# One-row last piece of w4: sixteen loads of eight partitions in place of one load of 128

## The chip, the cores and the metric

The kernel runs on one core of a Trainium2 chip. The metric is the device time of one execution in microseconds; the runs of the kernel before took 406.42, 406.50 and 406.69 us (median 406.5).

## What is computed

One decode step of a block with two branches that share an input row x of 1024 values:

```python
x = A_x                                   # (1, 1, 1024)
xn = _layernorm(x)
return x + _A_ref(xn, ...) + _B_ref(xn, ...)
# A: q = xn @ wq, 32 query heads over 4 key/value heads, 65536 cached keys of width 128,
#    softmax(q k^T / sqrt(128)) v, then @ wo (4096 x 1024)
# B: h = gelu(layernorm(xn) @ w1), shifted by rows (with one row, zeros come in), @ w2, added to xn = x1;
#    x1 + gelu(layernorm(x1) @ w3) @ w4,   w3 1024 x 3584, w4 3584 x 1024
```

All tensors are bf16. The caches are 64 MB each, the weights the rest of 170 MB that are read once. With one row the shifted operand is all zeros, and the kernel takes the layer norm of x1 as that of xn; the w2 product is computed nonetheless.

## The kernel before

Everything that is read from memory comes through one list of `items` (lines 82 to 91), in the order of their use: two halves of wq, then for each of four key/value heads four tiles of 16384 keys (K) and values (V), with w3 and w1 put in between and a piece of wo behind each head, and at the end w2 and w4. w4 (28 rows of 1024 for each of 128 partitions) is cut by `W4_PIECES = (16, 8, 2, 1, 1)` into five pieces: 4 MB, 2 MB, 0.5 MB and twice 0.25 MB. The text calls them piece 0 to piece 4.

Each item is one load into one buffer ("slot") of a pool of five, issued on SP's queue by `issue` (line 98). Before item i is computed, `ensure(i + 4)` issues the loads up to four items ahead (lines 129 to 132, 441). A load into a slot waits for the reads of the item that had the slot five places before, and for that item's own load. So piece 4 is issued when the w2 matmuls are done, piece 3 when those of the last wo are.

A framework puts the waits in. It tells the completion of DMAs issued on SP and ACT by eight semaphores, lane 0 to lane 7, that are given out in turn: in the kernel before w2 has lane 3, pieces 0 to 4 have lanes 4, 5, 6, 7 and 0, and the two stores of the output lanes 1 and 2. A DMA that gets a lane again must wait on its queue until the lane's earlier DMA has landed, if nothing it has waited for before implies this.

`compute_w4` (line 326) adds the pieces' products to the two output rows in PSUM: for each row of a piece two matmuls by `row_acc` (line 160), 56 in all, which share the accumulator `psB` with the products of wo and w2. After piece 4, ACT casts one half of the result (line 336) and VectorE the other (line 337), and ACT and SP store them (lines 339, 340).

Of the kernel before, what the change touches and what calls it, by code (L numbers as in the profile page):

```python
# [18 lines left out]
W4_PIECES = (16, 8, 2, 1, 1)  # L19
# [3 lines left out]
def kernel(  # L23
# [14 lines left out]
    nc = tc.nc  # L38
    P = 128
# [10 lines left out]
    NOUT = A_wo.shape[1]  # L50
# [24 lines left out]
    w4_v = B_w4.rearrange("(m c) n -> m c n", c=FC)  # L75
# [4 lines left out]
    w4_start = [sum(W4_PIECES[:i]) for i in range(len(W4_PIECES))]  # L80
# [12 lines left out]
    st = {}  # L93

    def slot():
        return big.tile([P, KEYS], BF16, name="slot")

    def issue(item):
        kind = item[0]
        t = slot()  # L100
        if kind == "wq":
            src = wq_v[:, 4 * item[1]:4 * item[1] + 4, :].rearrange("p c n -> p (c n)")
        elif kind == "w3":
            src = w3_v[:, 4 * item[1]:4 * item[1] + 4, :].rearrange("p c n -> p (c n)")
        elif kind == "w4":
            c0 = w4_start[item[1]]
            src = w4_v[:, c0:c0 + W4_PIECES[item[1]], :].rearrange("p c n -> p (c n)")
        elif kind == "w1":
            src = w1_v
        elif kind == "w2":  # L110
            src = w2_v
        elif kind == "wo":
            src = wo_v[item[1]]
        else:
            cache = A_k_cache if kind == "K" else A_v_cache
            _, g, r = item
            src = cache[0, g, r * KEYS:(r + 1) * KEYS, :].rearrange("(p k) d -> p (k d)", p=P)
        nc.sync.dma_start(out=t[:, 0:src.shape[-1]], in_=src)
        st[item] = t
# [9 lines left out]
    def ensure(upto):  # L129
        while n_issued[0] <= min(upto, len(items) - 1):  # L130
            issue(items[n_issued[0]])
            n_issued[0] += 1
# [85 lines left out]
    for cg in range(4):  # L218
        nc.vector.tensor_copy(out=selbig[:, cg, :].rearrange("p (hl dd) -> p hl dd", dd=16),
                              in_=sel32[:, 8 * cg:8 * cg + 8].unsqueeze(2).to_broadcast([P, 8, 16]))  # L220
    sel8big = const.tile([P, P], F32, name="sel8big")
    nc.vector.tensor_copy(out=sel8big[:].rearrange("p (hl dd) -> p hl dd", dd=16),
                          in_=sel8[:].unsqueeze(2).to_broadcast([P, 8, 16]))
# [3 lines left out]
    for b in range(2):  # L227
        for par in range(2):
            nc.vector.tensor_copy(out=psel[:, 2 * b + par, :].rearrange("p (a i) -> p a i", a=4),  # L229
                                  in_=iv[:, b, par, :].unsqueeze(1).to_broadcast([P, 4, 32]))  # L230
# [242 lines left out]
```

## Time and profile before

| | before |
|---|---|
| runs (us) | 406.42, 406.50, 406.69 |
| profiled execution | 406.69 us, of which the span of its instructions is 404.8 |
| mean granted TensorE clock | 0.796 |
| PE busy | 245.7 us (61%), 1400 matmuls |
| VectorE busy | 215.7 us (53%) |
| ACT busy, POOL busy | 37.7 us, 11.2 us |
| moved by DMA | 170.11 MB, mean 420 GB/s over the span |
| first of the w4 matmuls, last of them, first cast of the output | 393.26, 400.76, 401.18 us |

Times in the views are microseconds from the start of the span. A line of the chain or the timeline has the start, the duration, the engine, the line of the kernel and the operation with its tiles (out<-in); "SPq" and "ACTq" are the queues that issue DMAs, and their durations are those of the issue, not of the transfer. "slot<-in_B_w_dram" are loads of w1 to w4. "DMA" in the page's rows is the mean busy share of sixteen DMA engines. A DMA of 128 partitions leaves sixteen semaphore updates in the trace, one for each engine that carried it; its landing is the last of them.

### The profile page before, as it was taken

What the parts mean: (1) busy time and instruction counts of PE and PEld (TensorE: products, weight loads), DVE (VectorE), ACT (ScalarE), POOL (GpSimd) and SP (SyncE); (2) the same over time, 40 slices, a digit from 0 to 9 for tenths busy, and PEclk for the clock granted to TensorE, in tenths of its full rate; (3) what the DMA queues carried; (4) which work ended last, traced back from release to release, by engine and by line L of the source; (5) the groups of instructions that cost most, each with busy time, mean ns of one, the idle gap of its engine ahead of it and who ended that gap; (6) DMA issues with size and microseconds to landing.
All of it is one profiled execution on the core that took longest, in us unless ns stands there. A gap on an engine that the chain in (4) does not pass through costs nothing.

```text
span 404.8 us, 3326 instructions
## 1 busy us (share of the span) xinstructions
PE 245.7 (61%) x1400; PEld 95.7 (24%) x1400; DVE 215.7 (53%) x235; ACT 37.7 (9%) x60; POOL 11.2 (3%) x30
## 2 busy tenths in 40 slices
PE   0385565328475847557657948384659474758456
PEld 0132222103132312112223313131233121213122
DVE  0419474017484848346665847475748383838500
ACT  0101101100201010120210010101010101010100
POOL 5001000000000000000010000000000000000000
PEclk9998878857795778768595868888958797679898
DMA  8999999999999999999999999999999999999993
GB/s 363 415 424 449 418 426 434 430 418 444 434 408 439 447 416 419 458 418 416 447 431 413 437 444 414 435 440 418 430 440 424 428 439 427 425 437 413 440 415 134
DMA packets 7065, 170.11 MB, mean 420 GB/s; under 512 B 1023, under 2 KB 1033, under 8 KB 1418
## 3 DMA queue, kind: packets, MB, share of 16 engines
q1 hardware_dynamic: 6772, 169.87, 98.0%
q8 instruction: 11, 0.18, 0.2%
q0 software_dynamic: 128, 0.02, 0.0%
q10 hardware_dynamic: 150, 0.01, 0.0%
q14 instruction: 4, 0.03, 0.0%
HBM read 169.88 MB, written 0.01 MB: 420 GB/s over the span
## 4 chain that ended last, share of the span: by engine, by line
DMA 54%; PE 23%; DVE 17%; ACT 2%; another core or an unknown queue 1%; issue 1%; DVEq 0%; ACTq 0%
DMA slot<-in_A_k_cache_dram 44%; DVE slot L353 11%; PE sc L357 10%; DMA slot<-in_B_w_dram 7%; PE psB L160 5%; PE oacc L389 4%; DMA x_bf<-in_A_x_dram 3%; DVE pT L377 2%; DVE mx L361 2%; ACT p_sb L374 2%; PE rows L244 1%; PE pm_e L417 1%; DVE m L365 0%; PE pm_mx L363 0%
## 5 line engine op out<-in xcount | busy, mean ns | idle before, releaser
L353 DVE STREAM_TRANSPOSE slot<-slot 128x2048 f32<-128x2048 f32 x64 | 142.3, 2281 | 61.1 <-DMA slot<-in_A_k_cache_dram 61.1
L357 PE MATMUL sc<-slot,qst 128*128 128x512 bf16 x512 | 131.6, 411 | 40.9 <-DVE slot L353 40.9
L389 PE MATMUL oacc<-slot,pT 128*32 128x512 bf16 x512 | 56.0, 616 | 48.0 <-DVE pT L377 48.0
L357 PEld LDWEIGHTS <-qst 128*128 128x128 bf16 x512 | 51.6, 103 | 125.1 <-issue 45.9
L361 DVE TENSOR_REDUCE mx<-sc 128x1 f32<-128x1024 f32 x16 | 19.6, 1225 | 34.7 <-PE sc L357 34.7
L374 ACT ACTIVATE p_sb<-sc,nball 128x1024 bf16<-128x1024 f32 x16 | 17.8, 1114 | 209.8 <-DVE nball L372 209.8
L389 PEld LDWEIGHTS <-pT 128*32 128x32 bf16 x512 | 17.5, 139 | 75.0 <-DVE pT L377 49.4
L377 DVE STREAM_TRANSPOSE pT<-p_sb 128x1024 bf16<-128x1024 bf16 x16 | 19.9, 1245 | 23.3 <-ACT p_sb L374 23.3
L244 PE MATMUL rows<-slot,xpad 128*32 128x512 bf16 (+1 forms) x144 | 13.6, 509 | 6.1 <-DMA slot<-in_B_w_dram 6.1
L363 PE MATMUL pm_mx<-ident_f,mx 128*1 128x128 f32 x16 | 4.3, 270 | 21.1 <-DVE mx L361 21.1
L160 PE MATMUL psB<-slot,oT 128*1 128x512 bf16 x64 | 12.6, 564 | 4.3 <-DVE oT L428 4.3
L394 ACT COPY ob<-oacc 128x512 f32<-128x512 f32 x12 | 7.0, 586 | 58.6 <-PE oacc L389 58.6
L160 PE MATMUL psB<-slot,dst_h 128*1 128x512 bf16 x56 | 7.9, 444 | 3.2 <-DMA slot<-in_B_w_dram 3.2
L370 PE MATMUL pm_mx<-ident_f,rep 1*128 1x1 f32 x16 | 3.5, 222 | 9.9 <-DVE rep L367 9.9
L417 PE MATMUL pm_e<-og,selbig 128*128 128x128 f32 x32 | 7.4, 403 | 3.4 <-DVE og L409 3.4
L244 PEld LDWEIGHTS <-xpad 128*32 128x32 bf16 x144 | 5.7, 127 | 15.0 <-issue 13.7
L172 PE MATMUL pm_ln<-ln_rowsum_a,ones_f 128*128 128x1 f32 x2 | 0.6, 348 | 13.6 <-DVE psel L229 13.6
L337 DVE CAST out<-psB 64x256 bf16<-64x256 f32 x1 | 0.4, 417 | 15.2 <-ACT out L336 15.2
L363 PEld LDWEIGHTS pm_mx<-ident_f,mx 128*1 128x1 f32 x16 | 1.3, 79 | 29.0 <-DVE mx L361 29.0
L417 PEld LDWEIGHTS pm_e<-og,selbig 128*128 128x128 f32 x32 | 6.3, 293 | 6.7 <-DVE og L409 6.7
L365 DVE TENSOR_REDUCE m<-pm_mx 1x8 f32<-1x128 f32 x16 | 4.4, 278 | 5.8 <-PE pm_mx L363 5.8
L374 ACT ACT_TABLE_LOAD x3 | 3.8, 1283 | 35.6 <-DVE nball L372 35.6
(97 smaller groups left out, 79.3 us busy)
## 6 DMA issues: line engine op xcount, KB each, us to landing
slot<-in_A_k_cache_dram SPq DMA_DIRECT2D x16, 4096.0 KB, 34.5
slot<-in_A_v_cache_dram SPq DMA_DIRECT2D x16, 4096.0 KB, 35.5
slot<-in_A_wq_dram SPq DMA_DIRECT2D x2, 4096.0 KB, 21.4
slot<-in_A_wo_dram SPq DMA_DIRECT2D x4, 2048.0 KB, 38.4
slot<-in_B_w_dram SPq DMA_DIRECT2D x2, 3584.0 KB, 42.6
slot<-in_B_w_dram SPq DMA_DIRECT2D x3, 2048.0 KB, 26.9
slot<-in_B_w_dram SPq DMA_DIRECT2D x1, 4096.0 KB, 27.8
slot<-in_B_w_dram SPq DMA_DIRECT2D x1, 512.0 KB, 16.1
```

The costliest lines, as they stand in the source:

```text
L160: nc.tensor.matmul(psB[32 * j:32 * j + 1, :], lhsT=lhsT, rhs=rhs, start=(not row_started[j]), stop=False, tile_position=(0, 32 * j), skip_ ...
L244: nc.tensor.matmul(acc[32 * j:32 * j + 32, bk, 0:width], lhsT=xp[:, c, :], rhs=wt[:, cl, ch * width:(ch + 1) * width], start=(c == 0), sto ...
L353: nc.vector.transpose(out=kf[:, cg, :], in_=kf[:, cg, :])
L357: nc.tensor.matmul(sc[:, hf, :], lhsT=qst[g % 2][:, o:o + 128], rhs=kr[:, cg, hf, :, bp // 2, :, bp % 2], start=(cg == 0 and bp == 0), sto ...
L361: nc.vector.reduce_max(out=mx[:], in_=sc[:].rearrange("p h n -> p (h n)"), axis=AX.X)
L363: nc.tensor.transpose(pm[0:1, 0:P], mx[:, 0:1], ident_f[:])
L365: nc.vector.reduce_max(out=m8[:], in_=pm[0:1, 0:P].rearrange("o (j h) -> o h j", h=8), axis=AX.X)
L374: nc.scalar.activation(out=p_sb[:], in_=sc[:], func=ACTF.Exp, bias=nball[:, r:r + 1], scale=SCALE, accum_out=lall[:, r:r + 1])
L377: nc.vector.transpose(out=pT[:], in_=p_sb[:])
L389: nc.tensor.matmul(oacc[32 * u:32 * (u + 1), :], lhsT=pT[:, hf, 32 * t:32 * (t + 1)], rhs=vt[:, :, hf, t, :], start=(hf == 0 and t < 4), s ...
L394: nc.scalar.copy(out=ob[:], in_=oacc[:])
L417: nc.tensor.matmul(pe[:, 0:P], lhsT=selbig[:, cg, :], rhs=og[:, 128 * cg:128 * (cg + 1)], start=(cg == 0), stop=(cg == 3))
```

## The change

Piece 4 is no longer loaded by one DMA of 128 partitions x 2 KB, but by sixteen, each of eight partitions x 2 KB: for each block of 32 partitions (`base`), four loads that take every fourth partition from `base + s` on. The text calls them part 0 to part 15. The slot, the bytes and the matmuls are the same.

```diff
+        elif kind == "w4" and item[1] == len(W4_PIECES) - 1:
+            c0 = w4_start[item[1]]
+            for base in range(0, P, 32):
+                for s in range(4):
+                    sl = slice(base + s, base + s + 29, 4)
+                    nc.sync.dma_start(out=t[sl, 0:NOUT], in_=w4_v[sl, c0, :])
+            st[item] = t
+            return
         elif kind == "w4":
             c0 = w4_start[item[1]]
             src = w4_v[:, c0:c0 + W4_PIECES[item[1]], :].rearrange("p c n -> p (c n)")
```

In the built program nothing else changes its place on any engine. On SP the sixteen parts stand where the one load stood, with lanes 0 to 7 twice over:

```
part  0          waits for the w2 load and the w2 matmuls, as the one load did     lane 0
parts 1, 2, 3    no wait                                                           lanes 1, 2, 3
part  4          waits for lane 4, piece 0                                         lane 4
part  5          waits for lane 5, piece 1                                         lane 5
part  6          waits for lane 6, piece 2                                         lane 6
part  7          waits for lane 7, piece 3                                         lane 7
parts 8 to 15    wait for lanes 0 to 7, parts 0 to 7                               lanes 0 to 7
```

On TensorE the weight load ahead of piece 4's first matmul waits for lanes 1 to 7 and that matmul for lane 0; before, the matmul alone waited, for lane 0. The output's stores now have lanes 0 (ACT) and 1 (SP) and wait for parts 8 and 9.

## The prediction

> **What bounds the kernel now.** I read the page first: the DMA row is at 9 in nearly every slice and 3 in the last, and the chain that ended last is 54% DMA. So the body runs at the pace of the loads, and the change can only act at the end, where the chain in order of time shows what is last:
>
> ```profile
> DMA  8999999999999999999999999999999999999993
> DMA 54%; PE 23%; DVE 17%; ACT 2%; another core or an unknown queue 1%; issue 1%; DVEq 0%; ACTq 0%
> ...
> 365.42 27.79 DMA slot<-in_B_w_dram
> 393.21 0.04 issue
> 393.26 7.49 PE psB L160 x54
> 400.75 0.01 issue
> 400.76 0.40 PE psB L160 x2
> 401.15 0.02 issue
> 401.18 0.38 ACT out L336
> ```
>
> TensorE waits for piece 0 of w4 until 393.2, runs 54 matmuls, then the last two (piece 4) at 400.76, and the output follows. The chain draws 393 to 401 as TensorE's own work, so I looked next at what the loads do beside it, in a table of stretches (PE and PEld busy, then clock, DMA share, GB/s at the end of each line), and at the landings:
>
> ```profile
> 396.20:397.20 1.00, 1.00 (x12) 0.46 (x10) 0.00 (x0) 0.00 (x0) 0.00 (x0) 0.94 1.03 395
> 397.20:398.20 1.00, 1.00 (x12) 0.37 (x10) 0.00 (x0) 0.00 (x0) 0.00 (x0) 1.00 0.60 217
> 398.20:399.20 1.00, 1.00 (x12) 0.44 (x11) 0.00 (x0) 0.00 (x0) 0.00 (x0) 1.00 0.34 129
> 399.20:400.20 1.00, 1.00 (x14) 0.39 (x10) 0.00 (x0) 0.00 (x0) 0.00 (x0) 1.00 0.18 66
> 400.20:401.20 1.00, 0.93 (x8) 0.20 (x4) 0.00 (x0) 0.02 (x1) 0.00 (x0) 1.00 0.00 0
> ...
> slot<-in_B_w_dram SPq DMA_DIRECT2D x2, 256.0 KB, 11.1
> ```
>
> The share falls from 1.03 to 0.18 over three microseconds: the sixteen DMA engines don't finish together. The trace's semaphore updates give the same per load: each leaves sixteen, and the last of them is at 393.22 for piece 0, 398.15 for piece 1, 399.39 for piece 2, 400.07 for piece 3 and 400.72 for piece 4 (first of piece 4: 397.35). Piece 4 lands 0.04 us ahead of its matmuls. Pairs of matmuls run 0.216 us apart just before, and the last pair comes 0.39 after the one before it. So the end hangs on piece 4's last landing, by 0.17 us only; any delay of that landing moves the end one for one.
>
> Last, what issuing costs SP (start, duration of the issue):
>
> ```profile
> 0.74 0.88 SPq L118 DMA_DIRECT2D slot<-in_A_wq_dram  x2
> 1.66 0.43 SPq L118 DMA_DIRECT2D slot<-in_A_k_cache_dram  x1
> 2.13 0.71 SPq L118 DMA_DIRECT2D slot<-in_A_v_cache_dram  x1
> 2.89 0.44 SPq L118 DMA_DIRECT2D slot<-in_A_k_cache_dram  x1
> ...
> 343.55 0.33 SPq L118 DMA_DIRECT2D slot<-in_A_wo_dram  x1
> ...
> 402.02 0.63 SPq L340 DMA_DIRECT2D out_dram<-out  x1
> ```
>
> A load of 128 rows is issued in 0.33 us when alone, in about 0.43 back to back at the start, 0.04 to 0.07 apart. The two output stores, of two rows each, took 0.63 (SP) and 0.61 (ACT, alone when it began).
>
> **The change, part by part.** *Removed:* one issue of 0.33 us at 390.11 and its 128 packets of 2 KB.
>
> *Added:* sixteen issues of eight rows. What matters is what they wait for. The program hands the completion semaphores of SP's and ACT's DMAs out of eight lanes in turn. A DMA that takes a lane again waits, on its issuing queue, until the lane's earlier DMA has landed. Loads five places back have been waited for anyway, which is why the kernel before shows no such wait. In the built program part 0 waits as piece 4 did, parts 1 to 3 for nothing, part 4 for piece 0, part 5 for piece 1, part 6 for piece 2, part 7 for piece 3, and parts 8 to 15 for parts 0 to 7. SP works in order, so everything behind a waiting part waits too.
>
> *The sum,* on the clock of the span. Parts 0 to 3 go out from 390.11, part 4 at 393.25, part 5 at 398.2, part 6 at 399.4. All of this lies beside loads that are in flight and costs nothing: rings are drained in order, as the landings of pieces 1 to 4 show, and the parts stand behind piece 3. Part 7 can't start before 400.07, when piece 3 has landed; with SP's wake-up, 400.1. Then parts 8 to 15 follow back to back: eight pitches, with nothing to hide them.
>
> - Pitch: at least 0.33 + 0.04 = 0.37 us, by the issues alone; as much as 0.71 + 0.04 = 0.75, by the longest. I take 0.61 + 0.04 = 0.65, by the output stores, the only hardware-queue DMAs of the trace, beside the one-row x load (0.54 against 0.42 for the 128-row one), with under sixteen rows. Also, the built program marks every load on SP as prepared ahead, and neither the stores nor the sixteen parts. Eight pitches: 5.2 us (3.0 to 6.0). Part 15 starts at 405.3.
> - From issue to landing, with idle DMA engines: the stores were issued at 401.57 and 402.02, and their packets show in the DMA row 1.23 us later, the 7s of this line over 402.0 to 404.8, in slices of 0.07 us:
>
> ```profile
> GB/s 0 0 0 0 0 0 0 0 0 0 0 7 7 0 0 0 0 7 7 0 0 0 0 0 0 0 0 0 0 0 0 0 0 0 0 0 0 0 0 0
> ```
>
>  To that come one 2 KB packet (85 ns, the median of piece 3's and piece 4's) and the way from the last packet of piece 4 (ends at 400.27) to its last landing (400.72), 0.44: 1.23 + 0.09 + 0.44 = 1.76 us. The stores landed 1.60 after issue, which is the lower end; I allow 2.0 above, for a read from memory that the stores don't have. Part 15 lands at 407.1. Parts 8 to 11 wait for parts 0 to 3, which land right behind piece 3 (four packets of 85 ns: by 400.4), part 15 for part 7, landed at about 401.9: neither adds.
> - TensorE: the weight load ahead of the last two matmuls waits for seven lanes and the matmul for the eighth, where one wait stood before. SP's waits of this kind at the end of the trace come 0.06 us apart; the three or so that follow part 15's lane add 0.1 us.
> - The casts and stores after it are the same. The stores now wait for lanes of parts 8 and 9, landed before; behind SP's parts only SP's store is queued, and it waits for VectorE anyhow.
>
> Sum: 407.1 − 400.7 + 0.1 = 6.4 us (ends: 4.0 with pitch 0.37 and 1.60, 7.5 with 0.75 and 2.0). The profiled execution took 406.69, its span 404.8 and 1.9 around it; it is the highest of the three runs, 0.2 over the median of 406.5. It goes to 413.1, the median to 413.0.
>
> *A rule against the sum's size.* The row is the store's 1.60 us from issue to landing for 1 KB. The Trainium skill (DMA: Bandwidth & Descriptors, Anatomy of one DMA) fits a fixed 2.0 us plus the bytes over 436 GB/s to DMAs issued from GpSimd; an estimate by it is 2.04 for 16 KB, and the sum would be 6.7. The same page (Rules for kernel authors) advises coalescing transfers under 64 KB, which speaks against this change; the trace has no SP load that small.
>
> **The rivals.** *Cheap issues:* the parts cost what the prepared loads do, 0.37 to 0.55 a pitch. For: they too are plain loads, of the same queue. Against: the stores and the one-row load. 400.1 + 3.0 to 4.4 + 1.76 gives 410.7 to 412.2; 410.2 with a landing of 1.60 and no more.
>
> *Dear issues:* over 0.75 a pitch, up to 1.0, if an unprepared issue of eight rows costs more than one of two. 413.8 to 415.8. Against: a whole 128-row issue is 0.33.
>
> *The last bytes only go to fewer engines:* the stores of two rows left two landings, so eight rows plausibly use eight DMA engines. If the waits didn't hold back the parts, each of the eight would carry sixteen packets behind piece 3, 16 × 85 ns = 1.4 us, landing at 401.4: 407.3. This needs parts 7 to 15 issued before 400, against the built waits. The Trainium skill (DMA: Bandwidth & Descriptors, Why a DMA increments its semaphore by 16) has such a rule: the engines used are the largest number up to 16 that divides the row counts, the lowest-numbered first; the two landings agree.
>
> *Not slower:* the table shows engines idle from 397.2 on. If the parts were all issued by about 398 (1.8 us ahead of 400) and spread to the engines that are early, piece 4 would be in before TensorE comes to it; TensorE then runs on at its 0.216 pace and the end comes 0.17 earlier: 406.3. It decides from the point where part 15 is issued before 398.8. For: SP is idle from 390.5 to 402. Against: part 5 waits for piece 1, at 398.15.
>
> **How the numbers follow.** Forecast 0.60 (pitch 0.55 to 0.75: 412.2 to 413.8), cheap 0.22, dear 0.10, fewer engines only 0.03, not slower 0.03, something unseen 0.02. The range goes from 410.2 to 414.8, which leaves out the upper half of the dear case and the last three: some 0.13. A measurement of this kernel tells about 0.2% (0.8 us) from no change: the two cases near 406 to 407 count as same, so faster 0.02, same 0.05, slower 0.93. Most of the chance lies on one side because the gate of part 7 and the eight issues behind it stand in the built order, and no row hides them.
>
> **What would show it.** Right: SP's row shows parts 0 to 3 from 390, part 4 near 393.3, part 5 near 398.2, then an unbroken row of issues from 399.4 to about 406, at 0.65 each; TensorE stops before its last two matmuls for some 6 us, put down to the DMA; everything up to 400.5 keeps its times. Wrong: the issues short or long (the pitch), a landing more than 2 us after the last issue, parts 5 to 7 issued before pieces 1 to 3 land, or piece 1 to 3 landing later than now because the parts crowd them.

## The result, and the profile after

The changed kernel takes 413.5 us (413.39 to 413.7 in four runs) against 406.55 (406.42 to 406.69): 1.0171 times the time before, 95% interval 1.0159 to 1.0183, or 6.95 us more. The profiled execution took 413.44 us with a span of 411.6; before it was 406.69 and 404.8.

The chain of waits of the changed kernel, in order of time over the last 14 us (start, duration, what):

```profile
388.01 11.94 DMA slot<-in_B_w_dram
399.96 0.03 issue
399.99 0.62 SPq L110
400.61 0.04 issue
400.66 0.62 SPq L110
401.28 0.04 issue
...
404.66 0.62 SPq L110
405.29 0.04 issue
405.33 1.90 DMA slot<-in_B_w_dram
407.23 0.14 issue
407.37 0.61 PE psB L168 x2
407.98 0.02 issue
408.00 0.38 ACT out L344
```

Where the kernel before went from TensorE straight into the cast (401.18), the chain now runs through SP: piece 3 lands at 399.96, part 7 is issued, eight more issues follow with 0.04 us between them, the ninth of the row at 405.33 is part 15, and it lands at 407.23. The cast starts at 408.00, 6.8 later.

The waits at the end, of the computing engines and of SP's queue (who waits, for whom, us in total, times, longest), and stretches of the new gap (TensorE's granted clock, DMA share and GB/s at the end of each line):

```profile
PE psB L168 <- DMA slot<-in_B_w_dram: 10.2, 2, 6.9
```

```profile
SPq L110 <- DMA slot<-in_B_w_dram: 5.5, 3, 4.3
```

```profile
401.20:403.20 2.00, 0.00 (x0) 0.00 (x0) 0.00 (x0) 0.00 (x0) 0.00 (x0) 0.90 0.11 25
403.20:405.20 2.00, 0.00 (x0) 0.00 (x0) 0.00 (x0) 0.00 (x0) 0.00 (x0) 0.50 0.09 25
405.20:407.20 2.00, 0.00 (x0) 0.00 (x0) 0.00 (x0) 0.00 (x0) 0.00 (x0) 0.50 0.09 25
407.20:408.20 1.00, 0.59 (x2) 0.11 (x2) 0.00 (x0) 0.20 (x1) 0.00 (x0) 0.50 0.00 0
```

TensorE waits once more than before, 6.9 us for the parts. For six microseconds nothing computes and the DMA engines are a tenth busy: the time is neither bandwidth nor arithmetic, it is one queue issuing. Meanwhile the granted clock falls to 0.50.

### The profile page after: what moved, and what is told of

Read it like the earlier page. It is cut to its first block, busy times and chain, and to the rows that moved or that the text cites. A ratio compares the mean times of both kernels' runs of the same rounds, so it can differ in the third digit from the quotient of the medians.

```text
span 411.6 us, 3345 instructions
## 1 busy us (share of the span) xinstructions
PE 245.7 (60%) x1400; PEld 94.8 (23%) x1400; DVE 215.7 (52%) x235; ACT 37.7 (9%) x60; POOL 11.2 (3%) x30
## 4 chain that ended last, share of the span: by engine, by line
DMA 58%; DVE 22%; PE 15%; ACT 2%; SPq 1%; issue 1%; another core or an unknown queue 1%; DVEq 0%; ACTq 0%
DMA slot<-in_A_k_cache_dram 51%; DVE slot L361 16%; PE sc L365 6%; DMA slot<-in_B_w_dram 3%; PE oacc L397 3%; DMA x_bf<-in_A_x_dram 3%; PE psB L168 2%; DVE pT L385 2%; DVE mx L369 2%; ACT p_sb L382 1%; PE rows L252 1%; SPq L110 1%; PE pm_e L425 1%; DVE og L417 0%
## 5 line engine op out<-in xcount | busy, mean ns | idle before, releaser
L365 PE MATMUL sc<-slot,qst 128*128 128x512 bf16 x512 | 133.6, 414 | 40.7 <-DVE slot L361 40.5
L168 PE MATMUL psB<-slot,oT 128*1 128x512 bf16 x64 | 10.9, 503 | 4.3 <-DVE oT L436 4.3
L425 PE MATMUL pm_e<-og,selbig 128*128 128x128 f32 x32 | 6.5, 364 | 3.4 <-DVE og L417 3.4
```

Of the source, the lines that this page charges most:

```text
L168: nc.tensor.matmul(psB[32 * j:32 * j + 1, :], lhsT=lhsT, rhs=rhs, start=(not row_started[j]), stop=False, tile_position=(0, 32 * j), skip_ ...
L365: nc.tensor.matmul(sc[:, hf, :], lhsT=qst[g % 2][:, o:o + 128], rhs=kr[:, cg, hf, :, bp // 2, :, bp % 2], start=(cg == 0 and bp == 0), sto ...
L425: nc.tensor.matmul(pe[:, 0:P], lhsT=selbig[:, cg, :], rhs=og[:, 128 * cg:128 * (cg + 1)], start=(cg == 0), stop=(cg == 3))
```

## The experiments

The theory: part 7 waits for piece 3 to land, because its completion lane does; SP works in order, so eight issues then follow with nothing beside them; a last landing and two matmuls end the kernel. The rivals: an issue is dear for another reason, the bytes on fewer DMA engines are slow, or many small loads cost the time wherever they stand. The sixteen parts of the changed kernel were never run without any wait; twelve_split, below, comes nearest to that. Apart from pool_pieces and taper40, all edits are to the loop that issues piece 4; the diffs are cut to the lines that differ.

| kernel | part 7 issued | issues behind it | apart | last landing | cast | time (us) |
|---|---|---|---|---|---|---|
| changed | 399.99 | 8 | 0.67 | 407.23 | 408.00 | 413.5 |
| sixteen_contig | 399.85 | 8 | 0.34 | 404.13 | 404.89 | 410.45 |
| twelve | 400.02 | 4 | 0.64 | 404.61 | 405.23 | 410.57 |
| sp_act | 400.08 | 4 on each queue | 0.67 | 404.95 | 405.72 | 411.24 |
| eight16 | 400.34 | 0 | | 402.09 | 402.64 | 408.17 |
| four_strided | no part 7 | | | 400.95 | 401.51 | 406.54 |
| before | one load | | | 400.72 | 401.18 | 406.55 |

The landings are the last of a load's semaphore updates in the trace. In sp_act the part that waits for piece 3, shown in the second column, is part 6, and part 14 is the last to be issued, since the lanes are given out in another order there. Wherever a part waits for piece 3 the row of this table adds up to the end: wait, issues, 1.6 to 2.2 us from the last issue to its landing, 0.55 to 0.77 to the cast.

**Neighbouring partitions (sixteen_contig).**

```diff
-                    sl = slice(base + s, base + s + 29, 4)
+                sl = slice(8 * s, 8 * s + 8)      # s in 0..15
```

> Sixteen parts of eight partitions each, but neighbouring partitions in place of every fourth; lanes and waits as in the changed kernel. Theory (part 7 waits for piece 3, then eight issues in a row on SP, with the issue dear because the partitions are strided): SP issues 0.40 to 0.45 us apart in place of 0.67, so 1.8 to 2.2 us less than the changed kernel, 411.3 to 411.7. Rival 1 (an issue is dear because eight rows use fewer than sixteen DMA engines): still 0.67 apart, 413.5. Rival 2 (the bytes on eight DMA engines are the cost): 413.5.

Measured: 410.45 us (1.0098 times before, 1.0083 to 1.0113). Its chain:

```profile
399.83 0.02 issue
399.85 0.27 SPq L109
400.12 0.04 issue
400.17 0.29 SPq L109
...
402.53 1.59 DMA slot<-in_B_w_dram
```

The issues fall from 0.62 to 0.29 us, more than expected, with the number of rows, of DMA engines (eight landings for each part, as in the changed kernel) and of bytes unchanged. Of the changed kernel's 6.95 us, 3.05 hangs on how dear an issue is: 2.7 in eight pitches, 0.3 in the last landing, which is counted from the start of its issue. Both rivals that left 413.5 are out. Two things changed with this edit, though: the step over the partitions, and the mark of loads prepared ahead, which these parts have in the built program and the strided ones haven't. two64, below, bears on that.

**Fewer parts (twelve).**

```diff
+            for lo, step, n in [(32 * b + s, 4, 8) for b in range(2) for s in range(4)] + [(64 + s, 4, 16) for s in range(4)]:
+                sl = slice(lo, lo + step * (n - 1) + 1, step)
```

> Twelve strided parts: eight of eight partitions as in the changed kernel, then four of sixteen (every fourth of the upper 64). Theory: the same wait for piece 3 ahead of part 7, four issues behind it in place of eight: four pitches of 0.67 less than the changed kernel, 410.8; and since sixteen_contig showed the partition step, not the number of DMA engines, to make an issue dear, the sixteen-partition parts too take 0.6 to 0.65 us each to issue. Rival (the price goes with fewer than sixteen DMA engines): the last four take 0.3, 409.6.

Measured: 410.57 us (1.0099, 1.0084 to 1.0114). After 400.02 its chain has four more issues:

```profile
400.02 0.62 SPq L109
400.65 0.04 issue
400.69 0.55 SPq L109
...
401.93 0.59 SPq L109
402.51 0.04 issue
402.56 2.06 DMA slot<-in_B_w_dram
```

Four issues fewer take 2.9 us off, four pitches of 0.67 being 2.7. Strided parts of sixteen partitions, on sixteen DMA engines and without the mark, still take 0.55 to 0.59; eight rows add 0.03 to 0.07 to that.

**Nothing behind part 7 (eight16).**

```diff
+                sl = slice(16 * s, 16 * s + 16)   # s in 0..7
```

> Eight parts of sixteen neighbouring partitions. Part 7 still waits for piece 3, but nothing is issued behind it, and sixteen DMA engines carry each. Theory (wait, then issues in a row): part 7 is issued at 400.0, lands 1.4 to 1.9 us later at 401.4 to 401.9, TensorE ends 0.8 to 1.3 later than before: 407.3 to 407.9. Rival (fewer DMA engines are the cost): as before, 406.5.

Measured: 408.17 us (1.0042, 1.0027 to 1.0056), 0.3 over the range. The chain shows the wait by itself:

```profile
388.60 11.73 DMA slot<-in_B_w_dram
400.33 0.02 issue
400.34 1.74 DMA slot<-in_B_w_dram
402.09 0.14 issue
402.22 0.40 PE psB L167 x2
```

Part 7 goes out 0.02 us behind piece 3's landing; with that one wait the kernel is 1.7 us over before. Some 0.3 of it is piece 3 itself, which lands 0.3 later than before in this profile; see neighbouring blocks below. TensorE's last pair takes 0.40 here, against 0.61 in the changed kernel.

**Two queues (sp_act).**

```diff
+                    eng = nc.sync if s % 2 == 0 else nc.scalar
```

> The sixteen strided parts of the changed kernel, issued in turn on SP and on ACT. Theory (the issue is SP's own time): behind the wait for piece 3 each queue has four parts left, so four pitches of 0.67 fall away, 410.8, or 410.3 if ACT's last is ahead. Rival (both queues share what makes the descriptors, one issue at a time): eight issues in a row as now, 413.5.

Measured: 411.24 us (1.0116, 1.0101 to 1.0131), nearer to 410.8 than to 413.5: the issues of SP and ACT overlap, 0.62 to 0.80 us each. The last part goes out at 402.76, as expected, but takes 2.20 to land in place of 1.90. The rival of one issue at a time for both queues is out; the price is the queue's own time, for the most part.

**No wait for a piece in flight: four32, four_strided, two64.**

```diff
+ four32:        sl = slice(32 * s, 32 * s + 32)   # s in 0..3
+ four_strided:  sl = slice(s, s + 125, 4)         # s in 0..3
+ two64:         sl = slice(64 * s, 64 * s + 64)   # s in 0, 1
```

> Four parts of 32 neighbouring partitions: lanes 0 to 3, whose earlier loads have landed, so no part waits for a piece in flight. Theory: all four are issued by 392 and stand behind piece 3, time as before, 406.3 to 406.8. Rival (splitting costs by itself, by more landings to wait for and more descriptors): 0.5 us or more over before, 407.0 and up.

> As four32, but each part takes every fourth of the 128 partitions. No part waits for a piece in flight; the issues are dear (0.6 us) and end by 395, hidden. If four32's 0.8 us over before came from a block of 32 neighbouring partitions being written by sixteen DMA engines at once, this is back at 406.4 to 406.8. If it came from four landings in place of one, 407.1 to 407.4 again.

> Two parts of 64 neighbouring partitions, no wait for a piece in flight. If each further landing costs (0.78 for three more): 406.7 to 406.9. If a block of neighbouring partitions costs as such: 406.9 to 407.3. If only blocks of 32 or fewer do: 406.4 to 406.7.

Measured: four32 407.25 us (1.0018, 1.0008 to 1.0027), two64 407.25 (1.0017, 1.0008 to 1.0026), four_strided 406.54 (1.0, 0.9991 to 1.0009). So four32 missed the theory's range and lies in the rival's, while four_strided is where the theory has it, and two64 where blocks of neighbouring partitions cost as such. The timeline of SP in four_strided, four issues merged, and its chain:

```profile
393.83 2.46 SPq L109 DMA_DIRECT2D slot<-in_B_w_dram  x4
```

```profile
395.70 5.25 DMA slot<-in_B_w_dram
400.95 0.14 issue
401.09 0.40 PE psB L167 x2
```

Four dear issues, done by 396.3 with piece 3 landing at 400.13, cost nothing: splitting, striding, more landings and four lanes to wait for are free as long as the issues are hidden.

two64 also bears on what makes an issue dear. Its two parts are neighbouring partitions, but the built program leaves the mark off them, and they take what strided parts take:

```profile
393.34 0.56 SPq L109
393.90 0.05 issue
393.95 7.33 DMA slot<-in_B_w_dram
```

The second took 0.58. Over all kernels, loads of 8 to 40 rows with the mark took 0.27 to 0.43 us to issue, and those of 128 rows 0.33, but up to 0.71 at the start of the kernel. Without the mark 8 strided rows took 0.62, with up to 0.81 for the first of a row and beside a second issuing queue; 16 and 32 strided rows and 64 neighbouring ones took 0.55 to 0.60, the two-row stores 0.54 to 0.64. So it isn't the step alone that is dear, as I had come to think after sixteen_contig: the price goes with the mark, which strided parts lack. No kernel changes the mark by itself, so that what it stands for is the cause is not shown, and one load speaks against it as the whole: the one-row x load on ACT has the mark too in the built program and took 0.54. What decides whether a load gets the mark wasn't tried.

What four32 lost isn't the number of landings: two64 lost as much with two, and four_strided nothing with four. It goes with blocks of neighbouring partitions: in four32 and two64 piece 3, ahead of them, lands at 400.99 and 400.71, and single 16 KB packets of piece 1 take up to 0.88 and 0.90 us, against 0.62 in four_strided and before. Why is open. The Trainium skill (DMA: Bandwidth & Descriptors, The descriptor swizzle) gives the lower and the upper 64 partitions different write ports, so that a block inside one half would use half of them; no run here shows a port.

**Lifting the wait with all the parts: pool_pieces, parts_pool, twelve_split.**

```diff
+ pool_pieces:  pieces 1 to 3 by nc.gpsimd.dma_start, the sixteen parts on SP
+ parts_pool:   the sixteen parts by nc.gpsimd.dma_start, the pieces on SP
+ twelve_split: as twelve, the eight parts of 8 by nc.gpsimd.dma_start, the four of 16 on SP
```

> The sixteen strided parts of the changed kernel on SP, but pieces 1, 2 and 3 of w4 are issued from POOL, which has completion semaphores of its own. So no part waits for them: part 7 waits for piece 0 (393.2), and part 15 is issued eight pitches later, at 398.6. Theory (the wait for piece 3 puts the issues on the path): all parts land by 400.5 to 401, beside the pieces, and most of the 7 us is gone: 406.5 to 407.8, the upper end if POOL's loads start late or run slower. Rival (sixteen small loads cost the time wherever they stand, by landings, small packets or waits on TensorE): 412 and more.

Measured: 413.56 us (1.0171, 1.0156 to 1.0186), in the rival's range. But it doesn't decide: POOL's loads are served beside SP's, not behind, and piece 0 came 6 us late. The chain:

```profile
364.12 35.17 DMA slot<-in_B_w_dram
399.28 0.04 issue
399.33 8.86 PE psB L169 x56
```

Part 7 waits for piece 0, so the wait had only moved, from piece 3 to piece 0, at nearly the same time (399.3), and TensorE had all 56 matmuls still to do: they end at 408.19, 1.6 after the last part has landed (406.63).

> The sixteen strided parts of the changed kernel issued from POOL, the pieces from SP as in the kernel before. POOL's DMAs have completion semaphores of their own, so no part waits for a piece; POOL's loads took 0.53 to 0.54 us to issue in pool_pieces. Theory (the wait for piece 3 puts the issues on the path): issues from 390.1 at 0.58 to 0.75 us a part, the last at 399 to 401.5, landing some 2 us later, so 406.8 to 409, well under the changed kernel's 413.5, and TensorE waits for a part issued before 401.5. Rival (sixteen small strided loads cost 7 us wherever they stand): 412.5 and more.

Measured: 411.21 us (1.0114, 1.01 to 1.0128), between the two ranges. POOL's timeline (the idle time before an issue and what ended it in brackets) shows why:

```profile
392.43 3.99 POOL L110 DMA_DIRECT2D slot<-in_B_w_dram  x8 [183.08 <-PE psB L168]
398.11 0.51 POOL L110 DMA_DIRECT2D slot<-in_B_w_dram  x1 [1.70 <-DMA slot<-in_B_w_dram]
399.19 3.44 POOL L110 DMA_DIRECT2D slot<-in_B_w_dram  x7 [0.57 <-DMA slot<-in_B_w_dram]
```

POOL has eight completion semaphores as well. Part 8 waits for part 0, which took 5.4 us to land beside the pieces where I had reckoned with 2, part 9 for part 1, and seven issues of 0.49 then stand on the path. The same pattern on another queue.

> The same twelve strided parts as the kernel twelve (410.57 us), but the eight of eight partitions are issued from POOL and the four of sixteen from SP. Eight parts on POOL's own eight completion semaphores and four on SP's lanes 0 to 3: no part waits for a piece in flight, nor for another part. In parts_pool the first eight parts on POOL had all landed by 400.6. Theory (only the waits put the issues on the path): the last landing is that of piece 3's or POOL's last part, 400.6 to 401.2, so 406.4 to 407.2. Rival (many small strided loads cost the time by themselves, as packets, landings or waits on TensorE): 410 and more, as twelve.

Measured: 407.56 us (1.0025, 1.0016 to 1.0035), 0.4 over the range, but 3.0 under twelve, whose parts it has. SP's and POOL's issues all end by 396.1 and the chain goes from the last of them to a landing:

```profile
392.04 3.49 POOL slot L110 x7
395.53 5.88 DMA slot<-in_B_w_dram
401.41 0.20 issue
401.60 0.40 PE psB L168 x2
```

With no semaphore reused of a load in flight, three quarters of twelve's 4.06 us over before are gone. What is left shows in POOL's last part, which lands at 401.41, and in piece 3, now at 400.54. So small loads by themselves cost at most the 1.0 us that is left, and the rival that puts the whole price on them is out.

**A faster version? forty, taper40.**

```diff
+ forty:   for lo, hi in ((0, 40), (40, 80), (80, 120), (120, 128)):   sl = slice(lo, hi)
+ taper40: the same, and W4_PIECES = (8, 8, 4, 4, 2, 1, 1)
```

> Four parts of neighbouring partitions, three of 40 and one of 8, lanes 0 to 3: no wait for a piece in flight, and the bytes go to ten, or eight, DMA engines in place of sixteen. If these are ahead of the slowest ones, as the landings of the parts in the changed kernel suggest (the last landing of part 0 comes 1.1 us before that of piece 3, which stands ahead of it), piece 4 lands with or just after piece 3: 406.2 to 406.6. If what four32 lost (0.8 us over before) is the price of four landings to wait for, it comes here too: 407.0 to 407.4. If ten engines with more packets each are slower: 407.5 and up.

> The same four parts for the last row, and w4 in seven pieces (8, 8, 4, 4, 2, 1, 1), so that TensorE starts on w4 some 5 us earlier and is idle when the last piece lands. If the loads end as before, the end is the last landing plus two matmuls: 406.0 to 406.6; if more pieces cost landings as in four32: 407 and up.

Measured: 407.26 us (1.0017, 1.0005 to 1.0029) and 407.1 (1.0015, 1.0005 to 1.0024). Both lie where the rival of four32's loss has them. Forty's seven runs spread widely, from 406.41 to 408.33, so its loss is the least sure. In forty piece 3 lands at 400.41 and the four parts at 400.74, 400.97, 401.28 and 401.47, so the ten engines are no earlier, and with blocks of neighbours the kernel loses what four32 lost. No kernel here beats the one before; four_strided equals it.

## Why the prediction was right

It gave 413.0 us, 410.2 to 414.8, and 413.5 were measured. The sum was made of four terms, and each of them stands in the trace. The errors hardly cancel: the gate came 0.1 early, and the other three terms each measured a little more than forecast.

- *The gate:* part 7 at 400.1; it came at 399.99, 0.03 behind piece 3's landing. That part 4 goes out near 393.3 and part 5 near 398.2 held too: the trace has them at 392.97 and 397.89. Parts 0 to 3 were to land right behind piece 3, by 400.4; they landed at 398.87 to 399.40, ahead of its last landing. No issue waits for them then, so it cost nothing.
- *The pitch,* 0.65 from the output stores' 0.61, with bounds 0.37 and 0.75: measured 0.67, eight of them 5.3 in place of 5.2. The value was right and one of its two reasons wrong. I had put it on fewer than sixteen rows, with the one-row load and the stores as evidence, and on the mark of loads prepared ahead. sixteen_contig (eight rows with the mark, 0.29), twelve (sixteen without, 0.55 to 0.59) and two64 (64 without, 0.57) show that from 8 rows up the row count does little and that the price goes with the mark. So the stores were the right row to take because they lack the mark, as the parts do, and not because they have few rows. The one-row load is the exception: it has the mark in the built program and took 0.54, and no run takes that apart. For marked parts the rival of cheap issues would have been near: sixteen_contig took 410.45, under its 410.7, as 0.29 us an issue lies below the 0.33 that I had as the floor.
- *Issue to landing,* 1.76: measured 1.90. The fixed 2.0 us that the prediction quoted from the Trainium skill (DMA: Bandwidth & Descriptors, Anatomy of one DMA) for GpSimd's DMAs gives 2.04 by estimate and 6.7 as the sum. The kernels with idle DMA engines have 1.59 (neighbouring, eight rows), 1.74, 1.90, 2.06 and 2.20, so one constant doesn't cover them, and for this kernel the row was 0.14 short, the Trainium skill's rule 0.14 long. The one load of this kind that POOL issued with the DMA engines nearly idle, the last part of parts_pool, took 1.85. Counted from the end of the issue, the five are at 1.3 to 1.5 (1.27 in the changed kernel): most of the spread is the time of the last issue itself, which this term counts in.
- *TensorE:* 0.1 for the further waits; 0.14 passes from landing to matmul, against 0.04 before. Left out of the sum: the last pair took 0.61 in place of 0.40, because the granted clock had gone to 0.50 while TensorE waited. The kernels with a short wait (eight16, four_strided) keep 0.40, but so does twelve, where TensorE waited 4.1 us at the full clock; sixteen_contig, with 3.9, has 0.61. So the length of the wait alone doesn't decide it.

By the landings: 407.23 − 400.72 = 6.5, with 0.1 for the wait and 0.2 for the clock 6.8, the shift of the cast; forecast was 6.4. (As printed, 407.1 − 400.7 + 0.1 is 6.5, within the rounding of its terms. The range's lower end, 410.2, is 0.3 under what its own terms give, 406.5 + 4.0; nothing came near it.) The hidden part stayed hidden: the sixteen issues began at 389.74, piece 0 landed at 392.95 (393.22 before) and piece 3 at 399.96 (400.07 before). Between the two landings lie 7.01 us in place of 6.85, so parts 0 to 6 took at most some 0.2 us from the pieces.

The rival of fewer DMA engines was right in its premise (each part leaves eight landings from DMA engines) and without effect here, since the share of the DMA engines is a tenth while SP issues. "Not slower" needed part 15 out by 398.8; part 7 alone was out at 399.99.

## What to carry to other kernels

A load cut into more pieces than the program has completion semaphores free is no longer a set of loads that queue up behind each other: the first piece that reuses a semaphore waits, on the issuing queue, for a load in flight, and every issue behind it moves from beside the transfers to the end. So count the loads in flight and the pieces against the lanes, and price what stands behind the first reuse at issues times pitch plus a landing, here 0.67 us each and 1.9. Up to that number a split can be free (four_strided). Look also at which loads the built program marks as prepared ahead, since the marked parts' issues took about half as long here, and spread the parts over all partitions, since the kernels with blocks of 32 to 64 neighbours took 0.7 us more.

## What the runs showed of the hardware that I had not expected

- The issue of a DMA on SP took mostly 0.29 us for eight partitions with the mark of loads prepared ahead and 0.62 without; 0.31 to 0.43 and 0.55 to 0.60 for sixteen; 0.57 for 64 without, 0.33 for 128 with it. One row with the mark took 0.54, on ACT.
- With the last 256 KB in blocks of 32, 40 or 64 neighbouring partitions the kernels took 407.25 to 407.26 us, with four interleaved parts 406.54, and piece 3, ahead of the blocks, landed at 400.41 to 400.99 in place of 400.13.
- A load issued from POOL is served beside those that SP issued before it: 2.75 MB from POOL put off a 4 MB load of SP by 6 us, and a 16 KB part from POOL took 5.4 us to land while SP's loads ran.
- In the changed kernel the clock granted to TensorE fell to half 2.3 us into its wait for the parts, and its next two matmuls took 0.2 us longer. In twelve it stayed at full through a wait of 4.1 us.
